# A linear-attention and MLP kernel: w spread by two TensorE row groups, unit 4 loaded ahead of w_out, score matmuls issued in pairs, and a new set of planner costs

## The chip, the cores and the metric

The kernel runs on one core of a Trainium2 chip. The core has five engines with their own instruction streams: TensorE (PE, with its weight loads shown as PEld), VectorE (DVE), ScalarE (ACT), GpSimd (POOL) and SyncE (SP), which here issues nearly all DMAs. They work on SBUF, on the PSUM banks that TensorE writes, and on device memory. The metric is the device time of one execution in microseconds (us), as a median of five runs.

## The reference

There are 4 x 8 heads with 768 time steps and a head dimension of 48. Per head a state is decayed by `w` and gains `k v` in each step; the output adds the current step with a weight `u`. The result goes through an MLP with the activation called smelu.

```python
for t in range(S):
    cur = einsum('bhd,bhe->bhde', u[None] * kt, vt)
    y[:, :, t] = einsum('bhd,bhde->bhe', rt, state + cur)
    state = w[None, :, :, None] * state + einsum('bhd,bhe->bhde', kt, vt)
x = y.transpose(0, 2, 1, 3).reshape(B * S, H * D)          # 3072 x 384
h = x @ w_in                                               # 384 -> 2048
g = where(h >= 1, h, where(h <= -1, 0, (h + 1) ** 2 / 4))
out = g @ w_out                                            # 2048 -> 384
```

## The kernel before, in words

**Units and blocks.** The time steps are cut in chunks of 128. A unit is one chunk of one batch entry, all 8 heads: 24 units, in the order of chunks. Two units make a block of 256 rows for the MLP: 12 blocks.

**Attention of a unit.** K and R (float32, 128 x 384) are scaled by powers of w, `Winv` and `Wpow`, into bf16 (`f_kw`, L447, and `f_rw`, L451). The scaled pair is transposed to `RK`: for the first 8 units by TensorE (L469) with a copy out of PSUM (`f_rk`), for the others by a transposing DMA on SP (L488). Scores are eight matmuls of 48 rows (`f_at`, L499), each in the lower or the upper half of the array's rows, into two PSUM buffers; DVE multiplies them with a triangular mask (`f_mask`, L505). The output y collects the carried state (L556, not for the first chunk) and scores times V (L559). The current step's weight comes from a product P and four small matmuls for the first 8 units (`f_p`, `f_dg`, L515 and L521) and from two products on POOL and a sum on DVE for the others (`f_ku`, `f_red`, L535 to L541). V times that weight (`f_vd`, L546) is added to y (`f_x`, L571). The result x is transposed into `xT`, by TensorE (L581) for 8 units and by DMA (L589) for the others. The state T gains four matmuls (`f_st`, L607), is decayed on POOL (L618) and cast to `Tbd`.

**MLP.** Layer 1 has eight groups per block, each six matmuls of 256 columns (`layer1`, L644) and one squaring activation on ACT (L656): the middle branch of smelu, for all elements. Layer 2 has four groups per unit, each four matmuls of 384 columns (`layer2`, L667); a copy out of PSUM and one output DMA follow (L690). Row norms of x and column norms of w_in (`f_sq` to `f_ws`, L707 to L724, and `f_b2` to `f_b4`) bound the largest |h|; if the bound is over the limit, a branch at the end does the MLP again in full (L759). It is not taken for these inputs.

**What sets the order.** All instructions are recorded as operations (`P.op`) with engines, planned durations, dependencies and a due time; `Plan.run` lists them greedily, and the program is issued in that order. The due times and their corrections (`CFG["due"]`, `CFG["bias"]`) are constants. MLP groups have a late due time, so they fill PE wherever attention has nothing to issue. Buffers come from pools (`slots`): for PSUM, four banks `a` for attention, two `h`, two `o`. The matmuls on `zero` (L357) are fillers at the start that compute nothing.

**Loads.** SP issues loads in the order of `CFG["order"]`: U is a unit's K, R and V, I a quarter of w_in, O a quarter of w_out (each weight quarter 768 KB in float32, cast to bf16 in three or four pieces at L284). Eight DMAs may be out at once.

**Preparing w.** `w_row` is loaded to one partition, ACT takes its logarithm there (L327), a matmul with ones spreads it over 128 partitions (`f_lwb`, L333), and two exponentials make Winv and Wpow (L359, L360).

Of the kernel before, what the change touches and what calls it, by code (L numbers as in the profile page):

```python
# [16 lines left out]
    "order": "U0 U1 U2 U3 I0 I1 I2 I3 O0 O1 O2 U4 O3 U5 U6 U7",  # L17
    "soft": 8,
    "sw": False,
    "due": [12.12, 22.15, 27.93, 36.84, 35.31],  # L20
    "step": 12.04,
    "warm": 24.0,
    "steady": 45.0,
    "slack": 0.19,
    "split": 2,
    "bias": {
        "at": 1.0, "bd": -4.91, "c_uw": 1.38, "dg": 0.1, "ku": -0.0, "kw": 1.96, "ldVf": 1.45, "red": -0.75,
        "rk": 0.3, "rkk": -6.72, "rkr": -0.29, "rw": 1.99, "st": 0.57, "t": -0.92, "trd": 0.24, "trk": -2.87,
        "trr": -3.35, "tw": -0.9, "v": -0.89, "x2": -1.05, "xt": 2.62, "y": -2.02,
    },  # L30
}


class Buf:
    def __init__(self, pool):
        self.pool, self.users, self.slot, self.t = pool, [], None, None


class Op:
    def __init__(self, name, engs, fn, deps, uses, allocs, due, dma, after, nb, late):  # L40
# [3 lines left out]
        self.eng = self.start = self.end = None  # L44
        for b in self.uses + self.allocs:
            b.users.append(self)


class Plan:
# [13 lines left out]
    def place(self, o):  # L63
        got, t = [], 0.0
        for b in o.allocs:
            best = None
            for i, cur in enumerate(self.slots[b.pool]):
                if any(g[0] == b.pool and g[1] == i for g in got):
                    continue
                if cur is None:  # L70
                    free = 0.0
                elif all(u.start is not None for u in cur.users):
                    free = max(u.end for u in cur.users) + SEM
                else:
                    continue
                if best is None or free < best[0]:
                    best = (free, i)
            if best is None:
                return None
            got.append((b.pool, best[1]))  # L80
# [3 lines left out]
    def run(self):  # L84
# [5 lines left out]
        while todo:  # L90
            cand, gone = [], []
            for o in todo:
                if any(d.start is None for d in o.deps) or any(a.start is None for a in o.after):
                    if o.late is not None and free["PE"] > o.late:
                        gone.append(o)
                    continue
# [15 lines left out]
            for o in gone:  # L112
                todo.remove(o)
                for b in o.uses:
                    b.users.remove(o)
            if not cand and gone:
                continue
# [70 lines left out]
def kernel(  # L188
# [163 lines left out]
    for i in range(160):  # L352
        def f_wm(e, i=i):
            if wmb.t is None:
                get(wmb, [128, 128], F32)
# [457 lines left out]
```

## Time and profile before

| what | value |
|---|---|
| median of five runs | 180.46 us (180.18 to 181.15) |
| profiled execution | 180.56 us |
| its span, first to last instruction | 178.6 us |
| PE, ACT, DVE, POOL busy | 168.8, 115.6, 112.0, 105.4 us |
| first layer-1 group | 18.56 us |
| end of the last matmul | 173.48 us |
| issue of the last output | 174.28 us |

Times in the timeline are us from the start of the span. A matmul's shown length includes its way through the array, so neighbours overlap; what a group costs PE is the distance from its start to the next start. An arrow in brackets names what ended the idle time before an instruction. Fillers count as busy.

### The profile page before, as it was taken

The numbers are of one execution on the slowest core, as the hardware profiler recorded it, in microseconds if no ns is written. First come the engines' busy times: TensorE is split into PE (matmuls) and PEld (weight loads), VectorE is DVE, ScalarE is ACT, GpSimd is POOL, SyncE is SP. The second block draws the span as 40 slices with busy tenths as digits, with TensorE's granted clock in tenths as the row PEclk, the third lists the DMA queues.
The fourth block names the chain that finished last, engine by engine and source line by source line (L and its number), as shares of the span: only waits on it lengthen the run. The fifth ranks groups of instructions, "written<-read, shape, count | busy, mean of one in ns | idle before, by whom it ended". The sixth has DMA issues, their size and how long they took to land.

```text
span 178.6 us, 4705 instructions
## 1 busy us (share of the span) xinstructions
PE 168.8 (94%) x1808; PEld 127.0 (71%) x1808; DVE 112.0 (63%) x221; ACT 115.6 (65%) x257; POOL 105.4 (59%) x142
## 2 busy tenths in 40 slices
PE   7899989999989999999999999989999999999980
PEld 7689967776767777777777767766767767777740
DVE  6699974598999795777758855746766634100000
ACT  4359987744476985884976766767685456645520
POOL 8659571387795999778599749579775510000000
PEclk9999999999999999999999999999999999999999
DMA  5999999997989959979899989889998782111111
GB/s 112 202 213 317 398 343 336 232 194 156 214 195 195 177 122 204 182 170 195 173 191 172 158 174 187 201 169 194 188 182 166 167 242 60 32 44 48 44 48 56
DMA packets 105920, 31.50 MB, mean 176 GB/s; under 512 B 98978, under 2 KB 104356, under 8 KB 105892
## 3 DMA queue, kind: packets, MB, share of 16 engines
q1 hardware_dynamic: 105744, 31.04, 78.4%
q8 instruction: 16, 0.26, 0.6%
q14 instruction: 12, 0.10, 0.2%
q10 hardware_dynamic: 148, 0.10, 0.2%
HBM read 20.65 MB, written 4.72 MB: 142 GB/s over the span
## 4 chain that ended last, share of the span: by engine, by line
PE 65%; DVE 12%; DMA 9%; ACT 4%; POOL 3%; issue 3%; SPq 1%; DVEq 0%; ACTq 0%; POOLq 0%
PE h L644 27%; PE o L667 27%; DMA RK<-KR 4%; PE a L499 3%; DMA R<-in_r_dram 3%; PE o L357 3%; DVE AT L505 3%; DMA out_dram<-os 3%; DVE VD L546 2%; DVE x L571 1%; PE a L559 1%; DVE KR L451 1%; PE a L556 1%; DVE w_in_sb L284 1%; DVE RK L284 1%
## 5 line engine op out<-in xcount | busy, mean ns | idle before, releaser
L644 PE MATMUL h<-xT,w_in_sb 128*128 128x256 bf16 x576 | 77.8, 273 | 1.0 <-DVE w_in_sb L284 0.4
L667 PE MATMUL o<-w_out_sb,g 128*128 128x384 bf16 x384 | 77.0, 326 | 0.0
L656 ACT ACTIVATE g<-h 128x512 bf16<-128x512 f32 x96 | 56.6, 595 | 27.9 <-PE h L644 26.6
L644 PEld LDWEIGHTS <-w_in_sb 128*128 128x128 bf16 x576 | 54.4, 98 | 15.0 <-issue 0.7
L667 PEld LDWEIGHTS <-g 128*128 128x128 bf16 x384 | 35.1, 98 | 15.5
L505 DVE TENSOR_TENSOR AT<-a,umask 128x512 bf16<-128x512 f32 x48 | 31.1, 683 | 8.6 <-PE a L499 8.4
L546 POOL TENSOR_TENSOR VD<-V,dg 128x384 f32<-128x384 bf16 x18 | 16.0, 892 | 11.9 <-DVE dg L541 8.3
L571 DVE TENSOR_TENSOR x<-a,VD 128x384 bf16<-128x384 f32 x24 | 13.3, 554 | 11.8 <-PE a L559 8.4
L536 POOL TENSOR_TENSOR KU<-KU,R 128x384 f32<-128x384 f32 x16 | 17.6, 1103 | 2.4 <-DMA R<-in_r_dram 1.3
L451 DVE TENSOR_TENSOR KR<-R,Wpow 128x384 bf16<-128x384 f32 x20 | 17.7, 887 | 2.1 <-DMA R<-in_r_dram 2.0
L535 POOL TENSOR_TENSOR KU<-K,u_bc 128x384 f32<-128x384 f32 x16 | 18.2, 1139 | 1.2 <-DMA K<-in_k_dram 1.1
L597 ACT ACTIVATE x<-x 128x384 bf16<-128x384 bf16 x24 | 12.5, 523 | 6.6 <-DVE x L571 6.2
L284 DVE COPY os<-o 128x384 f32<-128x384 f32 (+1 forms) x6 | 3.1, 521 | 19.9 <-ACT os L284 18.7
L618 POOL TENSOR_TENSOR T<-T,wc 128x192 f32<-128x192 f32 x20 | 12.0, 602 | 5.9 <-ACT T L284 4.0
L447 POOL TENSOR_TENSOR KR<-K,Winv 128x384 bf16<-128x384 f32 x11 | 11.0, 999 | 5.4 <-DMA K<-in_k_dram 4.6
L357 PE MATMUL o<-zero 128*128 128x128 bf16 x156 | 13.0, 236 | 1.0 <-DVE zero L321 1.0
L284 ACT COPY os<-o 128x384 f32<-128x384 f32 (+1 forms) x19 | 8.9, 470 | 6.7 <-PE o L667 3.6
L614 DVE TENSOR_TENSOR T<-T,a 48x192 f32<-48x192 f32 x32 | 11.2, 349 | 2.8 <-ACT g L656 1.1
L284 ACT CAST V<-Vf 128x384 bf16<-128x384 f32 x19 | 9.6, 507 | 4.6 <-DMA Vf<-in_v_dram 3.0
L447 DVE TENSOR_TENSOR KR<-K,Winv 128x384 bf16<-128x384 f32 x13 | 9.3, 713 | 4.2 <-DMA K<-in_k_dram 4.1
L284 ACT CAST Tbd<-T 48x192 bf16<-48x192 f32 x30 | 10.4, 347 | 2.0 <-PE a L556 1.2
L357 PEld LDWEIGHTS <-zero 128*128 128x128 bf16 x156 | 10.6, 107 | 1.2 <-DVE zero L321 1.0
(78 smaller groups left out, 174.0 us busy)
## 6 DMA issues: line engine op xcount, KB each, us to landing
K<-in_k_dram SPq DMA_DIRECT2D x24, 192.0 KB, 3.7
R<-in_r_dram SPq DMA_DIRECT2D x24, 192.0 KB, 4.1
Vf<-in_v_dram SPq DMA_DIRECT2D x24, 192.0 KB, 4.5
out_dram<-os SPq DMA_DIRECT2D x23, 192.0 KB, 2.3
wf<-in_moe_w_in_dram SPq DMA_DIRECT2D x4, 768.0 KB, 7.6
wf<-in_moe_w_out_dram SPq DMA_DIRECT2D x4, 768.0 KB, 8.9
RK<-KR SPq DMA_TRANSPOSE x16, 3.2
xT<-x SPq DMA_TRANSPOSE x16, 3.0
```

Of the source, the lines that this page charges most:

```text
L284: (nc.scalar.copy if eng == "ACT" else V_ENG[eng].tensor_copy)(o, i)
L357: mm(wmb.t, zero, zero, start=True, stop=True, skip_group_check=True)
L447: V_ENG[e].tensor_mul(krb.t[:, H:, 0:D], Kb.t, Winv)
L451: V_ENG[e].tensor_mul(krb.t[:, :H, 0:D], Rb.t, Wpow)
L505: nc.vector.tensor_mul(atb.t[s], at_p[s].t, umask4)
L535: nc.gpsimd.tensor_mul(kub.t, Kb.t, u3)
L536: nc.gpsimd.tensor_mul(kub.t, kub.t, Rb.t)
L546: V_ENG[e].tensor_mul(vdb.t, vb.t, dgb.t[:, :, None].to_broadcast([128, H, D]))
L571: nc.vector.tensor_add(xb.t, yb.t[:, 0:384].rearrange("p (h d) -> p h d", h=H), vdb.t)
L644: mm(hb.t[:, f, :], w_in_sb[:, kk, (2 * n + f) * 128 : (2 * n + f + 1) * 128], xT[m][:, kk, :], start=(kk == 0), stop=(kk == nKb - 1),)
L656: nc.scalar.activation(gb[m].t[:, 2 * n : 2 * n + 2, :], hb.t, AF.Square, bias=0.5, scale=0.5)
L667: mm(ob.t, gb[m].t[:, f, j * C : (j + 1) * C], w_out_sb[:, f, :], start=(f == 0), stop=(f == nN - 1))
```

## The change

The new version differs in these parts:

- **w.** Its two halves are loaded to partitions 0 and 64 (`w_sp`). Two matmuls, each in its own row group, spread w itself over 128 partitions; ACT takes the logarithm of the spread halves, then the two exponentials. The rows for the per-partition constants are made afterwards.
- **Load order.** Unit 4 comes ahead of the first quarter of w_out instead of ahead of the last: on SP, the issues after w_in's last quarter are K4, R4, O0, V4, O1, O2, O3, K5, R5; before they were O0, K4, O1, O2, R4, O3, V4, K5, R5.
- **Blocks whole** (`split` 0). In units 0 and 1 the transposes and copies of K and R are issued as one, no longer as two halves.
- **Transposes.** Units 8 and 9 also use TensorE for `RK` (`tpe` 10); the xT transposes and the P path stay with the first 8 units.
- **First unit in any bank.** Unit 0 may use PSUM banks of all three pools (`wide` 1); the planner picks the bank that is free first.
- **Masks.** One of the two masks of units 0 and 1 is taken from a bf16 copy that ACT makes out of PSUM.
- **Pairs.** From block 4 on, the score matmuls of a block's two units are issued as one operation of sixteen, which takes all four `a` banks.
- **Norms of w_in.** POOL adds the two halves of each squared pair into `mx`; eight small matmuls come in one place instead of sixteen in eight places, and start 30 us later.
- **Output.** The last unit's layer 2 is cut into columns 0 to 255 and 256 to 383, each with its own PSUM buffer, eviction and output on SP. Units 12 to 17 send their rows in two DMAs.
- **Fillers** have 256 columns instead of 128. **The fallback branch** is a loop over chunks.
- **Planner.** It has new durations (a slower DVE where POOL is busy, slower matmuls before 5.5 us), due times and corrections, so that the order of nearly all instructions changes a little.

```diff
-    "order": "U0 U1 U2 U3 I0 I1 I2 I3 O0 O1 O2 U4 O3 U5 U6 U7",
-    "soft": 8,
+    "order": "U0 U1 U2 U3 I0 I1 I2 I3 U4 O0 O1 O2 O3 U5 U6 U7",
+    "tpe": 10,
+    "dmm": 8,
+    "xpe": 8,
+    "pair": 4,
+    "cold": 5.5,
+    "am0": 0,
+    "am1": 2,
+    "norm": 100.0,
+    "wide": 1,
-    "due": [12.12, 22.15, 27.93, 36.84, 35.31],
-    "step": 12.04,
+    "due": [6.87, 37.3, -17.41, 33.54, 38.54],
+    "step": 11.06,
-    "slack": 0.19,
-    "split": 2,
+    "slack": 0.05,
+    "split": 0,
...
-    zero = const.tile([128, 128], BF16, name="zero")
-    w_row = const.tile([1, H * D], F32, name="w_row")
+    zero = const.tile([128, 256], BF16, name="zero")
+    w_sp = const.tile([128, H * D // 2], F32, name="w_sp")
...
+    def f_wb(e):
+        for s in range(2):
+            get(wbb[s], [128, H // 2, D], F32)
+            mm(wbb[s].t, onesf[s * DP : s * DP + 1, :], w_sp[s * DP : s * DP + 1, :], start=True, stop=True)
+    c_wb = P.op("c_wb", {"PE": (0.45, 0.55)}, f_wb, deps=[c_wr, c_z], allocs=wbb, due=-98)
+    lws = [slice(s * H // 2, (s + 1) * H // 2) for s in range(2)]
+
+    def f_lw(e):
+        for s in range(2):
+            nc.scalar.activation(lw[:, lws[s]], wbb[s].t, AF.Ln)
...
-            for _ in range(2):
-                mm(wmb.t, zero, zero, start=True, stop=True, skip_group_check=True)
+            mm(wmb.t, zero[:, 0:128], zero, start=True, stop=True, skip_group_check=True)
...
+        A = "a h o" if i < CFG["wide"] else "a"
+        by_pe, by_mm, x_pe = i < CFG["tpe"], i < CFG["dmm"], i < CFG["xpe"]
...
+            if i < CFG["am%d" % s]:
+                amb = Buf("am")
+
+                def f_am(e, s=s, amb=amb):
+                    get(amb, [128, NP, 128], BF16)
+                    nc.scalar.copy(amb.t, at_p[s].t)
+                o_am = P.op(f"am{s}_{i}", act(512), f_am, deps=[o_at], uses=[at_p[s]], allocs=[amb], due=D0 - 3)
+
+                def f_mask(e, s=s, amb=amb):
+                    nc.vector.tensor_mul(atb.t[s], amb.t, umaskb4)
...
+        if m >= CFG["pair"]:
+            def f_at2(e, got=got):
+                for x in got:
+                    x[0](e)
+            o = P.op(f"at_{m}", pe(0.63), f_at2, deps=got[0][1] + got[1][1], uses=[x[2] for x in got], allocs=got[0][3] + got[1][3], due=got[0][4])
+            ats = [o, o]
...
+        cuts = [(0, d_out)] if i < NU - 1 else [(0, 256), (256, d_out)]
+        rows_ = [(0, C)] if i not in TWICE else [(0, C // 2), (C // 2, C)]
...
+            for k, (r0, r1) in enumerate(rows_):
+                def fo(e, lo=lo, hi=hi, r0=r0, r1=r1):
+                    nc.sync.dma_start(out=out[t0 + r0 : t0 + r1, lo:hi], in_=osb.t[r0:r1, lo:hi])
...
+            nc.gpsimd.tensor_add(mx[n // 2], ssb.t[:, 0:128], ssb.t[:, 128:256])
...
+    def f_np(e):
+        get(npb, [128, nP], F32)
+        for g in range(nP):
+            mm(npb.t[:, g : g + 1], mx[g], ones, start=True, stop=True)
...
+        with tc.For_i(0, NCH, 1) as ci:
```

## The prediction

> **What bounds the kernel now.** I read the page's busy line first, then its slices, then the chain of waits, and last TensorE's timeline.
>
> ```profile
> span 178.6 us, 4705 instructions
> PE 168.8 (94%) x1808; PEld 127.0 (71%) x1808; DVE 112.0 (63%) x221; ACT 115.6 (65%) x257; POOL 105.4 (59%) x142
> ...
> PE   7899989999989999999999999989999999999980
> ...
> DMA  5999999997989959979899989889998782111111
> ```
>
> PE is the busy engine, and the DMA engines are full for the first quarter. But a busy PE early on is partly filler: the matmuls on `zero` (L357) compute nothing. So I went through PE's timeline:
>
> ```profile
> 0.99 3.17 PE L357 MATMUL o<-zero 128*128 128x128 bf16 x28 [0.99 <-DVE zero L321]
> 4.09 1.18 PE L333 MATMUL a<-rows,onesf 1*128 1x384 f32 x2
> ...
> 18.56 0.82 PE L644 MATMUL h<-xT,w_in_sb 128*128 128x256 bf16 x6
> ...
> 25.81 2.33 PE L644 MATMUL h<-xT,w_in_sb 128*128 128x256 bf16 x18 [0.37 <-ACT w_in_sb L284]
> ...
> 35.77 0.82 PE L667 MATMUL o<-w_out_sb,g 128*128 128x384 bf16 x4
> ```
>
> The first layer-1 group starts at 18.56, the groups then wait for the casts of w_in (25.81), and the group at 35.77 is the first that uses the last quarter of w_out. The transfers set these, as the casts that waited for them show:
>
> ```profile
> 26.06 0.70 POOL L284 CAST w_out_sb<-wf 128x384 bf16<-128x384 f32 x1 [1.07 <-DMA wf<-in_moe_w_out_dram]
> 28.95 0.70 POOL L284 CAST w_out_sb<-wf 128x384 bf16<-128x384 f32 x1 [2.19 <-DMA wf<-in_moe_w_out_dram]
> 31.55 0.70 POOL L284 CAST w_out_sb<-wf 128x384 bf16<-128x384 f32 x1 [1.90 <-DMA wf<-in_moe_w_out_dram]
> 34.66 0.51 POOL L284 CAST w_out_sb<-wf 128x384 bf16<-128x384 f32 x1 [2.41 <-DMA wf<-in_moe_w_out_dram]
> ```
>
> So w_out's quarters land at 26.0, 28.9, 31.5 and 34.6. After 35.77 PE is the bound, and only less work or fewer waits on it help. The steps are read from start to next start:
>
> ```profile
> 146.84 0.81 PE L644 MATMUL h<-xT,w_in_sb 128*128 128x256 bf16 x6
> 147.59 0.40 PE L499 MATMUL a<-RK 48*128 48x128 bf16 x8
> 147.92 0.82 PE L667 MATMUL o<-w_out_sb,g 128*128 128x384 bf16 x4
> 148.58 0.60 PE L644 MATMUL h<-xT,w_in_sb 128*128 128x256 bf16 x4
> ```
>
> An MLP group steps 0.65 us (147.92 to 148.58). The group ahead of the 48-row score matmuls (L499) steps 0.75, so going into them costs 0.10, and the eight step 0.33: 0.43 for a unit. The same reading gives 0.44 for a unit's eight transposes, 0.11 for dg, 0.17 each for st, xp and the carried state in y, 0.20 for y's own eight. Last, the tail:
>
> ```profile
> 173.54 0.32 ACT L284 COPY os<-o 128x192 f32<-128x192 f32 x1 [2.12 <-PE o L667]
> 173.89 0.38 ACTq L690 DMA_DIRECT2D out_dram<-os  x1
> 173.89 0.36 DVE L284 COPY os<-o 128x192 f32<-128x192 f32 x1 [18.66 <-ACT os L284]
> ```
>
> PE ends at 173.48; the two half evictions run one after the other, and the last output is issued at 174.28. The execution took 180.56 (1.96 outside its span), 0.10 above the median 180.46; my sum starts from 180.56.
>
> **The change, part by part.**
>
> *Start.* Before, w lands at 2.19, its logarithm ends at 2.71, but the broadcast matmuls stand behind 28 fillers until 4.09, and Winv ends at 5.89. After, five fillers of 256 columns come first, then two row groups spread w itself (L333 took 1.03 for twice the columns: 0.5 side by side, which I take, 1.0 one after the other), then two half logarithms on ACT (about 0.34 each, from 0.52 for 384 columns) and the exponentials (0.58): Winv at about 4.5, 1.4 earlier. Then I followed the new order by DVE, which has kw and rw of units 0 and 1 (0.55 each where POOL is idle, 1.27 where it is not), RK1 0.69, masks 0.68 or 0.42 from a bf16 copy, P 0.42, x 0.55: x of unit 0 ends at 13.9 (before 13.99), unit 1 at 16.35 (17.17), its transposed copy, behind a mask and a w_in cast, at 17.85. First layer-1 group at 18.0, not 18.56: R1 lands at 6.5 and the w_in casts end at 17.8, so most of the 1.4 is lost to loads. Larger fillers cost nothing: they stand where PE waits anyway.
>
> A row bears on the early matmuls: the 28 fillers step 0.113 us, those after 5 us 0.056, while the page's granted clock shows full speed throughout. The Trainium skill (TensorE: Matmul & The Clock Gate, Part 1: The HAM clock gate) says that an array just woken runs at half clock for about 3.4 us; the fillers' steps agree, and it speaks against moving the broadcast from 4.09 to 2.2; by it the two would take 1.03 and not 0.5, and Winv would end at 5.0. The sum would not move by either, since R1 and w_in come later still.
>
> *Four units, then w_in, then unit 4, then w_out.* The first sixteen loads keep their order, so w_in's last quarter still lands at about 23.8 and the seventh layer-1 group can start at 24.6 (before 25.81). Unit 4's three loads now stand ahead of w_out's last three quarters, where two stood before. Single loads follow each other by 0.7 to 1.0 us, so the last quarter lands at about 35.4 instead of 34.6, its casts take 1.0 as before, and the group of 35.77 starts at 36.4. From 24.6 PE has ten layer-1 groups, three layer-2 groups (8.45) and unit 4 (1.69): done by 35.3, with 0.5 for the wait on R. About 1.1 us of waiting is thus new. In return dg, st, the carried state, y and xp of unit 4 (0.82) lie behind. Net gain at this point 0.82 - 0.63 = 0.2.
>
> *PE work from there on.* Both have 173 MLP groups left: 112.45. Before: transposes of three units 1.32, scores 19 x 0.43 = 8.17, dg 0.44, st 2.72, carried state 3.40, y 4.00, xp 0.68, norms and b3 0.67. Sum 133.85, against 137.71 measured: 3.9 us of waits. After: units 8 and 9 also go through PE, so transposes are 5 x 0.44 = 2.20. Scores of blocks 4 to 11 are issued in pairs: eight matmuls in two row groups side by side need 4 x 0.055 (a transpose's step) = 0.22, so 0.11 of the 0.33 and the 0.10 before it are the cost of going in and out; a pair pays it once: 0.21 + 2 x 0.22 = 0.65 instead of 0.86. Scores: 3 x 0.43 + 8 x 0.65 = 6.5. dg 0.33, st 2.55, carried 3.23, y 3.80, xp 0.51, norms in one place and b3 0.42. Sum 132.0. No row shows a pair; between no saving (0.86) and 0.65 I take 0.65, since each of 14 score groups in steady state shows the 0.10. So before, 35.77 + 133.85 + 3.9 = 173.5; after, if the waits stay 3.9, 36.4 + 132.0 + 3.9 = 172.3: 1.2 earlier (1.85 less work, of which 0.8 had been done before 36.4, and 0.6 lost at the start).
>
> *Waits.* The longest of the old ones are for transposing DMAs (0.4 to 0.5), an output buffer at 115 and the row norms at 132.8. Two transposing DMAs fewer and one place of norms speak for less; four PSUM buffers taken at once by a pair, and six outputs split in two (six more issues of 0.4 to 0.6 on SP, with the loads queued behind) for more. Bounds -2 to +4; I take 0. The masks through ACT (units 0 and 1), P, and the norms on POOL run on engines that idle there; if that cover fails, the masks cost ACT 0.6 each. First units in any bank cannot cost once layer 1 starts; before, it only removes waits.
>
> *Tail.* One eviction of 128 columns (about 0.27, from 0.32 for 192) stands between the last matmul and the last issue, in place of 0.80: -0.4. The split layer 2 is 16 x 0.108 + 16 x 0.055 = 2.61 against 2.60. The fallback branch becomes a loop and doesn't run: 0, within 0.5 both ways.
>
> Sum: 180.56 - 1.2 - 0.4 = 178.96; less the 0.10 by which that execution lies above the median, 178.9. That is my prediction.
>
> **The rivals.**
> 1. Slower: a pair needs all four `a` buffers. PE runs in order, so it stands until every mask, copy and x of earlier units has freed them, with MLP groups queued behind. For it: masks are 0.68 each and DVE is 63% busy. Against: about 2 us of MLP groups lie around each pair. Eight waits of one mask, 5.4 us, give 184.3; from 0.21 us a pair the gain is gone, from 0.27 it is slower.
> 2. No change: w_out comes later by all three of unit 4's loads, 2.4 us instead of 0.8. For it: the DMA engines are full there; against: two of the three were ahead of the last quarter before. 178.9 + 1.6 = 180.5.
> 3. Larger gain: the waits halve (3.9 to 2.0) because two transposing DMAs leave the full stretch: 177.0. Against: DVE is at 9.2 of 10 us from 50 to 60.
> 4. Row groups don't run side by side: Winv 0.5 later, hidden by loads, so still 178.9.
>
> **How the numbers follow.** My forecast with rival 4 has 0.50 (its own range 177.9 to 179.9), rival 1 0.20, rival 2 0.15, rival 3 0.15. A measurement of this kernel tells about 0.3% from no change: under 179.92 or over 181.0. Faster: 0.50 + 0.15 + a little of rival 2 = 0.66; same 0.14; slower 0.20. The range takes rival 3 to its middle and rival 1 up to 0.38 us a pair: 176.9 to 181.9.
>
> **What would show it.** First layer-1 group at about 18.0; the fourth layer-2 group, after a wait for w_out's cast, at 36 to 37; pairs stepping 0.55 with 0.75 for the group ahead; PE's end near 172.3; 0.4 from there to the last issue. I am wrong if groups ahead of pairs step far over 0.75 (rival 1), if w_out's last cast ends past 37.5 (rival 2), or if PE waits elsewhere from 36 to 60, where DVE is nearly full.

## The result: no faster, and the profile after

| | kernel before | changed kernel |
|---|---|---|
| median of all executions, us | 181.15 (79) | 182.23 (42) |
| lowest to highest, us | 179.18 to 184.05 | 178.98 to 184.41 |
| ratio, 95% interval | | 1.0013 (0.9988 to 1.0037) |
| profiled execution, us | 180.56 | 182.91 |
| its span, us | 178.6 | 181.0 |

The forecast was 178.9, 0.85% faster. The measurement shows no gain, and by the medians of all executions the changed kernel is 0.6% slower. Single executions of either kernel scatter by some 1.5% and fall into a faster and a slower state: the ratio compares the faster ones alone (median 181.05 for the changed kernel), and of its two profiled executions the one here, 182.91, is of the slower ones, the second, 182.67 (h3_after, in the last group of runs), of the faster. The second profile has its marks within 0.2 us of the first. The two profiled executions in the table lie 2.35 us apart, the medians 1.1.

The first lines of the page of the changed kernel, and its chain of work that ended last:

```profile
PE 170.1 (94%) x1762; PEld 128.9 (71%) x1762; DVE 111.7 (62%) x218; ACT 118.4 (65%) x261; POOL 105.7 (58%) x147
...
PE h L717 32%; PE o L751 31%; PE o L406 5%; PE a L537 3%; PE a L611 2%; DVE AT L555 2%; DVE P L567 2%; PE a L507 2%; DMA RK<-KR 2%; DVE VD L598 2%; PE a L608 2%; DMA w_sp<-in_w_dram 1%; PE a L659 1%; DVE x L623 1%; DVE KR L489 1%
```

PE is as busy as before. New is the third entry of the chain: 5% of it, some 8 us, are fillers (L406), which compute nothing; 7.2 of these lie in the first 24 us. TensorE's timeline (start, us, engine, line, operation, what it waited for) shows where they stand:

```profile
3.48 1.01 PE L369 MATMUL a<-w_sp,onesf 1*128 1x192 f32 x4 [1.16 <-DMA w_sp<-in_w_dram]
4.42 2.74 PE L406 MATMUL o<-zero 128*128 128x256 bf16 x12
7.08 1.01 PE L391 MATMUL a<-onesf,rows 1*128 1x1 f32 x8
8.03 1.03 PE L507 MATMUL a<-ident,KR 128*128 128x128 bf16 x8
8.85 1.70 PE L406 MATMUL o<-zero 128*128 128x256 bf16 x7
...
11.55 0.47 PE L537 MATMUL h<-RK 48*128 48x128 bf16 x8
...
12.88 2.14 PE L406 MATMUL o<-zero 128*128 128x256 bf16 x18
16.28 0.25 PE L573 MATMUL a<-uw,P 128*128 128x2 bf16 x4 [1.25 <-DVE P L567]
...
23.12 0.81 PE L717 MATMUL h<-xTa,w_in_sb 128*128 128x256 bf16 x6
```

The twelve fillers step 0.21 us from start to start, the eighteen later ones 0.11: up to about 11.7 us the array works at half rate. In the kernel before, its one-column matmuls step 0.06 from 5.1 on, here 0.11: there full rate had come by then. The first scores (L537) start at 11.55, the first layer-1 group at 23.1 instead of 18.56. The kernel before had its first scores at 10.10:

```profile
10.10 0.40 PE L499 MATMUL a<-RK 48*128 48x128 bf16 x8
```

Which of these rows follow on one another is told by the chain of waits of the first 24 us (start, us, what):

```profile
0.79 2.55 DMA w_sp<-in_w_dram
...
4.48 2.67 PE o L406 x12
...
9.06 1.49 PE o L406 x7
...
13.85 1.24 DVE AT L552
15.09 2.14 DVE P L567 x2
...
20.12 1.20 PE o L406 x11
```

Fillers are links of this chain, then a mask (1.24 us for a 0.43 us operation) and two products P (2.14 us for 0.84). Fillers are links again from 18.9 to 23.0, 2.8 us of them, now at full rate. These stand mostly where TensorE would wait: the last input of the first layer-1 group, unit 1's transposed x, is copied by 22.5 (0.35 us from 22.16 on VectorE), so that the fillers and scores behind that copy can have held the group back by at most 0.6. ScalarE's queue shows why w is late: issuing the two-partition load took 1.11 us (first line, changed kernel), against 0.53 for the one-partition load (second line, kernel before).

```profile
0.79 1.11 ACTq L329 DMA_DIRECT2D w_sp<-in_w_dram  x1
0.77 0.53 ACTq L294 DMA_DIRECT2D w_row<-in_w_dram  x1
```

Late in the kernel the pairs step as forecast, 0.55, and the group ahead of each steps 0.75. Two of the eight pairs have a wait inside (0.74 and 1.00). One of the other six:

```profile
61.76 0.82 PE L717 MATMUL h<-xTa,w_in_sb 128*128 128x256 bf16 x6
62.51 0.62 PE L537 MATMUL a<-RK 48*128 48x128 bf16 x16
63.06 0.82 PE L751 MATMUL o<-w_out_sb,g 128*128 128x384 bf16 x4
```

### The profile page after: what moved, and what is told of

Same layout as the page of the kernel before. It is cut to its first block, busy times and chain, and to the rows that moved or that the text cites. A ratio compares the mean times of both kernels' runs of the same rounds, so it can differ in the third digit from the quotient of the medians.

```text
span 181.0 us, 4588 instructions
## 1 busy us (share of the span) xinstructions
PE 170.1 (94%) x1762; PEld 128.9 (71%) x1762; DVE 111.7 (62%) x218; ACT 118.4 (65%) x261; POOL 105.7 (58%) x147
## 4 chain that ended last, share of the span: by engine, by line
PE 79%; DVE 12%; DMA 3%; ACT 1%; issue 1%; POOL 0%
PE h L717 32%; PE o L751 31%; PE o L406 5%; PE a L537 3%; PE a L611 2%; DVE AT L555 2%; DVE P L567 2%; PE a L507 2%; DMA RK<-KR 2%; DVE VD L598 2%; PE a L608 2%; DMA w_sp<-in_w_dram 1%; PE a L659 1%; DVE x L623 1%; DVE KR L489 1%
## 5 line engine op out<-in xcount | busy, mean ns | idle before, releaser
L717 PE MATMUL h<-xTa,w_in_sb 128*128 128x256 bf16 x576 | 76.8, 272 | 1.3 <-DMA xTa<-x 1.0
L751 PE MATMUL o<-w_out_sb,g 128*128 128x384 bf16 (+2 forms) x400 | 75.7, 320 | 0.0
L751 PEld LDWEIGHTS <-g 128*128 128x128 bf16 x400 | 36.6, 98 | 15.7
L555 DVE TENSOR_TENSOR AT<-a,umask 128x512 bf16<-128x512 f32 x45 | 28.3, 683 | 14.2 <-PE a L537 14.0
L598 POOL TENSOR_TENSOR VD<-V,dg 128x384 f32<-128x384 bf16 x19 | 15.9, 838 | 18.0 <-DVE dg L593 8.0
L489 DVE TENSOR_TENSOR KR<-R,Wpow 128x384 bf16<-128x384 f32 x22 | 16.7, 758 | 1.0 <-DMA R<-in_r_dram 0.8
L623 DVE TENSOR_TENSOR x<-a,VD 128x384 bf16<-128x384 f32 x24 | 13.3, 554 | 4.2 <-PE a L611 3.8
L406 PE MATMUL o<-zero 128*128 128x256 bf16 x84 | 14.5, 316 | 1.1 <-DVE zero L358 1.1
L319 ACT COPY os<-o 128x384 f32<-128x384 f32 (+2 forms) x21 | 9.7, 463 | 7.5 <-PE o L751 6.9
L319 ACT CAST Tbd<-T 48x192 bf16<-48x192 f32 x36 | 12.5, 346 | 2.2 <-POOL T L670 1.9
L593 DVE TENSOR_REDUCE dg<-KU 128x8 f32<-128x384 f32 x16 | 8.7, 546 | 7.1 <-POOL KU L588 7.0
L802 POOL TENSOR_TENSOR ss<-sq 128x256 bf16<-128x256 bf16 x8 | 5.7, 708 | 10.6 <-ACT sq L793 10.6
L406 PEld LDWEIGHTS <-zero 128*128 128x128 bf16 x84 | 8.5, 111 | 3.4 <-DVE zero L358 1.1
```

Source lines behind the costliest of these rows:

```text
L319: (nc.scalar.copy if eng == "ACT" else V_ENG[eng].tensor_copy)(o, i)
L406: mm(wmb.t, zero[:, 0:128], zero, start=True, stop=True, skip_group_check=True)
L489: V_ENG[e].tensor_mul(krb.t[:, :H, 0:D], Rb.t, Wpow)
L555: nc.vector.tensor_mul(atb.t[s], at_p[s].t, umask4)
L598: V_ENG[e].tensor_mul(vdb.t, vb.t, dgb.t[:, :, None].to_broadcast([128, H, D]))
L623: nc.vector.tensor_add(xb.t, yb.t[:, 0:384].rearrange("p (h d) -> p h d", h=H), vdb.t)
```

## The experiments

For every run I read four marks in TensorE's timeline: the first scores, the first layer-1 group, the fourth layer-2 group (the first that needs the last quarter of w_out), and PE's end (the end of its last matmul). "Rest" is from the fourth layer-2 group to PE's end. Times are medians of all executions of that batch, with the kernel before beside it; the ratio is against the kernel before.

| run | first scores | first L1 | fourth L2 | PE's end | rest | median (n) | before (n) | ratio, 95% |
|---|---|---|---|---|---|---|---|---|
| before | 10.10 | 18.56 | 35.77 | 173.48 | 137.7 | | | |
| h4_before | 9.97 | 18.4 | 36.0 | 172.1 | 136.1 | 179.90 (1) | 180.77 (11) | |
| after | 11.55 | 23.12 | 40.34 | 176.56 | 136.2 | 182.23 (42) | 181.15 (79) | 1.0013 (0.9988 to 1.0037) |
| h3_after | 11.54 | 23.25 | 40.44 | 176.39 | 136.0 | 183.31 (4) | 180.77 (11) | 1.018 (1.011 to 1.025) |
| e1_drop20 | 9.75 | 22.14 | 39.25 | 174.98 | 135.7 | 181.08 (10) | 181.64 (25) | 1.0014 (0.9967 to 1.0061) |
| e2_ahead5 | 11.26 | 22.98 | 40.33 | 177.02 | 136.7 | 182.00 (10) | 181.64 | 1.008 (1.002 to 1.014) |
| e3_onerow | 9.16 | 20.90 | 38.02 | 175.86 | 137.8 | 181.77 (10) | 181.64 | 1.007 (1.001 to 1.013) |
| e4_apart | 11.69 | 23.40 | 40.75 | 178.49 | 137.7 | 183.75 (4) | 181.64 | 1.017 (1.006 to 1.027) |
| f1_order | 11.55 | 21.94 | 39.06 | 174.32 | 135.3 | 182.42 (4) | 181.02 (25) | 1.012 (1.003 to 1.022) |
| f2_ahead14 | 11.38 | 22.90 | 40.02 | 175.84 | 135.8 | 181.65 (10) | 181.02 | 1.005 (1.000 to 1.011) |
| f3_order14 | 9.70 | 22.39 | 39.75 | 175.99 | 136.2 | 181.04 (10) | 181.02 | 1.005 (1.000 to 1.011) |
| f4_orderrow | 8.96 | 20.91 | 39.76 | 176.49 | 136.7 | 181.26 (10) | 181.02 | 1.0012 (0.9963 to 1.0061) |
| g1_late | 11.02 | 22.76 | 39.96 | 174.23 | 134.3 | 180.90 (4) | 180.60 (13) | 1.012 (1.001 to 1.023) |
| g2_new | 9.49 | 21.72 | 38.87 | 174.46 | 135.6 | 179.84 (10) | 180.60 | 1.0002 (0.9946 to 1.0059) |
| g2_again | 9.48 | 21.56 | 38.71 | 174.96 | 136.3 | 180.78 (12) | 180.42 (17) | 1.005 (1.001 to 1.010) |
| g3_newsp | 10.04 | 22.15 | 39.30 | 176.88 | 137.6 | 181.43 (4) | 180.60 | 1.011 (0.998 to 1.025) |
| h2_skip | 11.58 | 21.22 | 38.34 | 175.24 | 136.9 | 180.15 (1) | 180.77 | |
| h1_new2 | 9.48 | 18.30 | 42.56 | 178.26 | 135.7 | 184.11 (6) | 180.77 | 1.020 (1.014 to 1.026) |
| i1_new3 | 9.49 | 18.21 | 41.30 | 177.25 | 135.9 | 183.60 (12) | 181.57 (17) | 1.009 (1.005 to 1.013) |
| i2_new4 | 9.48 | 18.14 | 41.99 | 177.12 | 135.1 | 183.91 (6) | 180.42 | 1.024 (1.019 to 1.030) |

The rest lies between 134.3 and 137.8 whatever was edited at the start, and for the unedited kernels too (137.7 and 136.1 in two profiles of the one before). The same changed kernel gave 1.0013 in one batch and 1.018 in a batch of four. So a time of few executions can't tell effects under 1 us, and the verdicts below go by the marks. Each mark is of one execution: the two profiles of the changed kernel agree within 0.2, but where the moment of full rate differs the start moves by up to 1.9 (g1_late below). All edits keep the planner's list and change it, or a body, only when it is written out.

**Theory and rivals.** A: the fillers hold up the work behind them in TensorE's queue, at half rate above all. B: they only fill waits, and VectorE and GpSimd set the start. C: without them the array stays slow.

**e1_drop20: the fillers ahead of the first scores away.**

```diff
-    for o in P.run():
+    seq = P.run()
+    seq = [o for o in seq if o.name not in [f"wm{i}" for i in range(5, 25)]]
+    for o in seq:
```

> The changed kernel, its order kept, without the 20 fillers (256 columns each) that stand in TensorE's queue between the spread of w and the first scores (12 + 7 + 1, in its profile at 4.42 to 7.08, 8.85 to 10.35 and 11.20 to 11.55 us). Theory A, the fillers hold up the work behind them: the transposes of the u columns start when their rows are there (6.6, not 7.08), the second unit's transposes at about 8.9 (not 10.35), the first scores at about 9.7 (not 11.55), and with VectorE 1.8 us earlier from there the first layer-1 group comes at about 21.3 (not 23.1) and the time falls by 1 to 1.8 us. Theory B, they only fill waits and VectorE's and GpSimd's shared work sets the start: first layer-1 group within 0.4 of 23.1, the time the same. Theory C, they keep the array's clock up: without them the transposes and scores stay at half rate longer and the first layer-1 group comes later.

```profile
6.67 1.01 PE L391 MATMUL a<-onesf,rows 1*128 1x1 f32 x8 [2.16 <-ACT rows L379]
...
9.75 0.61 PE L537 MATMUL h<-RK 48*128 48x128 bf16 x8 [0.24 <-ACT RK L319]
...
11.90 4.02 PE L406 MATMUL o<-zero 128*128 128x256 bf16 x18
```

A holds for the first scores, 1.8 us earlier to within 0.1. The eighteen fillers that remain step 0.21, at half rate up to 15.9, and now stand ahead of a product that is ready. So the first layer-1 group gains 1.0, PE's end 1.6; the time does not differ from the kernel before. Whether the array stayed slow for so long because fillers were missing (C) is not shown by one execution: the moment of full rate moves without an edit too (g1_late below).

**e2_ahead5 and f2_ahead14: fillers moved ahead of the spread of w.**

```diff
+    for i in range(5, 10):
+        move(f"wm{i}", "c_wb")
```

```diff
+    for i in range(5, 14):
+        move(f"wm{i}", "c_wb")
+    k = seq.index(at["wm16"])
+    seq[k:k] = [at["wm15"]] * 13
```

> The changed kernel with five of the twelve fillers that follow the spread of w moved ahead of it, so that TensorE does not stand still from 2.3 to 3.5 us; as many fillers as before. If the pause is what keeps the array at half rate until about 11 us: full rate from about 4.1 us (as the unbroken fillers of the kernel before show), the spread 0.5 us, the later fillers 0.11 each, first scores at about 9 (not 11.55), first layer-1 group at about 20.6, time 1.5 to 2.5 us less. If the rate does not depend on the pause: only the five moved fillers (5 x 0.22 = 1.1 us) leave the queue ahead of the u columns, which then wait for their rows (6.6), and the gain is 0.5 us at most.

> The changed kernel with nine of the twelve fillers moved ahead of the spread of w, so that 14 fillers run unbroken from 1.07 to about 4.2 us, and 13 more fillers behind it to keep TensorE busy up to the u columns. If the array reaches full rate after about 3.1 us of matmuls over all its rows, as the 28 fillers of the kernel before do (0.99 to 4.09), and the one-row matmuls of the spread had broken that off: spread at 4.2 and 0.5 long, fillers 0.11 each behind it, transposes 0.45, first scores at about 9 (not 11.55), first layer-1 group at about 21.0 (not 23.1). If full rate comes at a fixed time from the start, or after the first transposes whatever came before: no change of the first scores beyond 0.5.

f2_ahead14 also puts thirteen more fillers behind the spread. The pause of TensorE at 2.3 us is not what keeps the rate down: with all but 0.45 us of it filled, fillers still step 0.21 to beyond 13 us, and the first three marks stay within 0.3. Nor do fourteen unbroken fillers ensure full rate: f2_ahead14 has no pause of TensorE from 1.07 to beyond 9 us, and half rate lasted to 9.4. The next two fences are f2_ahead14 and f3_order14 (below), whose instructions are the same up to the transposes:

```profile
1.07 3.17 PE L406 MATMUL o<-zero 128*128 128x256 bf16 x14 [1.07 <-DVE zero L358]
4.17 1.01 PE L369 MATMUL a<-w_sp,onesf 1*128 1x192 f32 x4
5.11 3.59 PE L406 MATMUL o<-zero 128*128 128x256 bf16 x16
```

```profile
4.17 0.88 PE L369 MATMUL a<-w_sp,onesf 1*128 1x192 f32 x4
4.98 1.92 PE L406 MATMUL o<-zero 128*128 128x256 bf16 x16
```

The sixteen fillers behind the spread step 0.21 in one execution and 0.11 in the other.

**e3_onerow: w in one partition, no row groups.**

```diff
-    c_wr = ... nc.scalar.dma_start(out=w_sp[0:128:64, :], in_=w.rearrange("(s h) d -> s (h d)", s=2)) ...
+    c_wr = ... nc.scalar.dma_start(out=w_row, in_=row(w)) ...
...
-            mm(wbb[s].t, onesf[s * DP : s * DP + 1, :], w_sp[s * DP : s * DP + 1, :], start=True, stop=True)
+            mm(wbb[s].t, onesf[0:1, :], w_row[:, s * (H * D // 2) : (s + 1) * (H * D // 2)], start=True, stop=True)
```

> The changed kernel with w loaded into one partition as in the kernel before and spread by two matmuls from that one row, one after the other; all else in its order. This undoes the row groups alone. If w's late landing and the pause of TensorE that it makes cost the start: w at 2.0 (not 3.3), the spread from about 2.3 without a pause before it, Winv at about 4.0 (not 5.07), full rate from about 4.1, first layer-1 group 2 to 3 us earlier and the time 1 to 2.5 us less. If two matmuls side by side were worth it: Winv no earlier than 5.0 and the time the same or up to 0.5 more.

```profile
2.25 1.64 PE L369 MATMUL a<-w_row,onesf 1*128 1x192 f32 x4
3.82 2.74 PE L406 MATMUL o<-zero 128*128 128x256 bf16 x12
...
9.16 0.40 PE L537 MATMUL h<-RK 48*128 48x128 bf16 x8
```

The load was issued in 0.51 us and the spread began 1.23 earlier. From one row it took 1.57 (2.25 to 3.82), from two row groups 0.94: these do run side by side, but the late landing costs more than they save, and Winv starts at 4.29 instead of 5.07. Full rate came at 7.0, the first layer-1 group 2.2 earlier, the fourth layer-2 group 2.3, PE's end only 0.7, since this execution has a rest of 137.8.

**g1_late: the one-row kernel without the late fillers.**

```diff
+    seq = [o for o in seq if not (o.name.startswith("wm") and o.start > 18.0)]
```

> w in one partition as in the one-row run, and besides without the fillers that stand behind the first layer-1 group's place and just ahead of it (from 18 us of the written order on: 8 + 2 stand between the first layer-1 groups at 22.6 and 25.1 of that run's profile, 1.1 us). If they hold up layer-1 groups that are ready: from the first layer-1 group (20.9) to the fourth layer-2 group 16.1 us instead of 17.1, which then comes at about 37, and the time falls by about 1 us against the one-row run. If the loads and casts of w_in and w_out set that stretch: fourth layer-2 group at 38 as before, no gain.

From the first layer-1 to the fourth layer-2 group it takes 17.2 us, as with the fillers: these do fill waits, for casts and evacuations. But this run tells more. Its first 17 us are written as in e3_onerow, and yet:

```profile
3.88 2.74 PE L406 MATMUL o<-zero 128*128 128x256 bf16 x12
...
8.32 1.70 PE L406 MATMUL o<-zero 128*128 128x256 bf16 x7
...
13.18 2.17 PE L406 MATMUL o<-zero 128*128 128x256 bf16 x18
```

Full rate came at 13.3, not 7.0, and the first layer-1 group at 22.76, not 20.90. So 1.9 us of the start are the moment of full rate, which is not the program's. Most of e3_onerow's gain is therefore that moment. Against the changed kernel, whose two profiles had full rate at 11.7 and 12.6, g1_late's first layer-1 group is only 0.4 to 0.5 earlier; that is what w's earlier landing is worth, as far as one execution shows it.

**h2_skip: VectorE without GpSimd beside it.** GpSimd's rw2, kw3 and rw3 are left out, so units 2 and 3 lack these values.

```diff
+    at["rw2"].fn = at["rw3"].fn = lambda e: None
+    at["kw3"].fn = lambda e: setattr(at["kw3"].allocs[0], "t", KR[at["kw3"].allocs[0].slot])
```

> The changed kernel without GpSimd's three products of units 2 and 3 that stand beside VectorE's masks and products of units 0 and 1 (rw2, kw3 and rw3, at 13.8 to 17.1 us in the profile after); the output lacks these units' keys and receptances. If the shared work slows VectorE: the second bf16 mask 0.43 (not 1.24) and the two products P 0.42 each (not 1.17), so that from the first scores to the first layer-1 group it takes 9.3 us instead of 11.6. If VectorE's order alone makes that stretch long: 11 or more.

VectorE's timeline of the changed kernel, then of this run:

```profile
13.85 1.24 DVE L552 TENSOR_TENSOR AT<-am,umaskb 128x512 bf16<-128x512 bf16 x1
15.01 2.35 DVE L567 TENSOR_TENSOR P<-RK 128x512 bf16<-128x512 bf16 x2
```

```profile
13.84 0.42 DVE L552 TENSOR_TENSOR AT<-am,umaskb 128x512 bf16<-128x512 bf16 x1
14.18 0.75 DVE L567 TENSOR_TENSOR P<-RK 128x512 bf16<-128x512 bf16 x2
```

The first scores are at 11.58 as before, the first layer-1 group at 21.22: 9.6 us between them instead of 11.6. It is the cleanest result of the study: 1.9 us of the start are GpSimd's work beside VectorE's. That units 2 and 3 need not wait for their own values here is no rival: in the changed kernel none of TensorE's waits before 23 us is for GpSimd. The Trainium skill (GPSIMD Engine Reference, 1. Specifications) says that the two engines' SBUF interface is shared and contends with VectorE instructions that have two SBUF inputs; the rows agree, since P and the mask from the bf16 copy take 2.5 to 3 times as long and the mask from PSUM (0.68 beside GpSimd) does not. GpSimd's timeline of the changed kernel shows how:

```profile
13.81 1.00 POOL L489 TENSOR_TENSOR KR<-R,Wpow 128x384 bf16<-128x384 f32 x1
14.76 1.17 POOL L485 TENSOR_TENSOR KR<-K,Winv 128x384 bf16<-128x384 f32 x1
15.90 1.17 POOL L489 TENSOR_TENSOR KR<-R,Wpow 128x384 bf16<-128x384 f32 x1
```

Each of the three VectorE operations starts just after one of these has started, and ends 0.28 us after that one's end (15.09, 16.22 and 17.36 after 14.81, 15.94 and 17.08). So it is not slower throughout, it is held until GpSimd's operation is done. In f1_order a P that starts 0.29 ahead of a GpSimd product takes its 0.42.

**f1_order, f3_order14 and f4_orderrow: products ahead of masks.**

```diff
+    behind("v0", "P0")
+    behind("at0", "dg0")
+    behind("am1_0", "dc0")
+    behind("kw2", "rw2")
+    behind("mask1_0", "P1", "vd0")
+    behind("wm33", "y0", "x0")
+    behind("wm39", "tr2", "xp0")
```

A name is an operation and its unit: `P0` is the product P of unit 0, `at0` its scores. f3_order14 adds the edit of f2_ahead14, f4_orderrow that of e3_onerow.

> The changed kernel with the first two units' work in another order and nothing else: the products P of units 0 and 1 stand ahead of the masks on VectorE (behind v0, and behind the first unit's masks), dg0, its copy, vd0, y0 and x0 follow at once, and GpSimd does rw2 ahead of tw0. Theory D, the order on VectorE costs the start (P at 15.0 to 17.4 us in the profile after, 1.17 us each beside GpSimd's kw and rw, 0.42 each in the kernel before): P0 at about 10.4, x0 at about 14.6 (not 18.5), first layer-1 group at about 20.7 (not 23.1). Theory A alone (TensorE's cold queue sets all of it): first layer-1 group within 0.6 of 23.1. For the time, 1 to 2 us less under D, none under A.

> Both edits, the order of the first two units and the 14 fillers ahead of the spread. If the start was lost by these two and the gain behind it is real, first layer-1 group at about 18.5, fourth layer-2 group at 36.5 to 37.5 (the last quarter of w_out lands at 36.05 in the profile after), PE's end at about 172.5 to 173.5 and the time 178 to 179.5: about the forecast. If the loads give the block-0 time back: fourth layer-2 group at 38 or later, time within 1 us of the changed kernel.

> The new order of the first two units together with w in one partition (no row groups), fillers as in the changed kernel. The one-row start alone had the first layer-1 group at 20.90. If the two causes add: about 18.5, fourth layer-2 group 36.5 to 37.5, time 178 to 179.5. If VectorE is what both wait for, so that they overlap: 20 to 20.5, time about 180.

The order alone gains half of what was expected (21.94, not 20.7). VectorE's sum for x of unit 0 starts 3.6 earlier (14.91, not 18.50), that for unit 1, which the group needs too, only 1.2 (19.58, not 20.76): GpSimd still holds up one P and one mask (1.02 and 1.11), and I had put unit 0's transposes ahead of unit 1's work, where they wait for x. In f3_order14, with full rate at 4.8 and the first scores at 9.70, that wait is longest:

```profile
15.96 0.34 PE L633 MATMUL h<-ident,x 128*128 128x128 bf16 x3 [1.45 <-DVE x L623]
```

Its first layer-1 group came at 22.39, not 18.5 as expected, and later than in f1_order. With w in one partition the order gains nothing more either: 20.91 against the 20.90 of e3_onerow. The causes do not add. In f4_orderrow w_out's last quarter landed at 38.74, and the fourth layer-2 group waited for its cast:

```profile
39.76 2.11 PE L751 MATMUL o<-w_out_sb,g 128*128 128x384 bf16 x12 [1.49 <-DVE w_out_sb L319]
```

In the other runs it landed between 35.5 and 37.8 and this wait is absent. So the loads are next in line: an earlier start helps only down to about the landing plus 1 us (39.76 after 38.74 in this one execution).

**e4_apart: the pairs taken apart.**

```diff
+            if m >= CFG["pair"] and j == 1:
+                mm(at_p[0].t[:, 0, 0:32], zero[:, 0:128], zero[:, 0:32], start=True, stop=True)
             for p in range(NP):
```

> The changed kernel with a matmul over all 128 rows (32 columns) put between the two units of each of the eight pairs of scores, so that the array leaves the half-row mode and enters it again once more a pair. If the pairs' saving is on the path that sets the end: 8 x (0.21 + about 0.05) = 2.1 us more. If waits had hidden it: under 0.5 us more.

```profile
62.91 0.40 PE L539 MATMUL a<-RK 48*128 48x128 bf16 x8
63.24 0.19 PE L536 MATMUL a<-zero 128*128 128x32 bf16 x1
63.37 0.40 PE L539 MATMUL a<-RK 48*128 48x128 bf16 x8
63.70 0.82 PE L753 MATMUL o<-w_out_sb,g 128*128 128x384 bf16 x4
```

Two units now take 0.79 instead of 0.55: 0.24 a pair, 1.9 in all. The rest, 137.7, does not decide, since e3_onerow has 137.8 without this edit; nor does the time (1.017, against 1.0013 and 1.018 of the unedited kernel). PE's busy time within the rest does: 135.9 us, against 134.0 and 133.9 in the two profiles of the changed kernel and 133.4 to 135.0 in all its other variants. The 1.8 to 2.0 more agree with the step, and PE stands still for only 1.9 of the 137.7: the pairs' saving is real and on the path.

**g2_new, g3_newsp and g2_again: a new order of the first four units.** The list is sorted anew with 29 operations given other places (products ahead of masks, v0 and vd0 to GpSimd, two copies to ScalarE), and most fillers are left out; g3_newsp has w over two partitions.

```diff
+    when = {
+        "P0": 8.17, "dg0": 8.3, "dc0": 8.85, "rw2": 9.05, "vd0": 9.06, "mask0_1": 9.6, "P1": 9.62, "y0": 9.63,
...
+    for n, e in (("v0", "POOL"), ("vd0", "POOL"), ("dc1", "ACT"), ("xt1", "ACT")):
+        at[n].eng = e
...
+    seq.sort(key=lambda o: o.start)
```

> w in one partition, and the first four units' work written in a new order: products ahead of masks, v0 and vd0 to GpSimd, two small copies to ScalarE, x1 and its transposes ahead of units 2 and 3, and two fillers of three left out from 10 us on, all from 18. This asks whether the first layer-1 group can stand at the 18.0 of the forecast, and what the whole kernel then takes. If the start is all that failed in the forecast: first layer-1 group at 17.5 to 18.5, fourth layer-2 group at the last landing of w_out (36 to 37.5) plus about 1, PE's end 172 to 173.5, time 178 to 179.5. If the start is worth little because w_out's landing and the casts on VectorE come next: fourth layer-2 group at 38 or later, time 180 to 181.

> The same new order with the two row groups of the changed kernel (w over two partitions). Against the run with w in one partition it shows what the row groups cost in an order that is not held up elsewhere: if w's later landing (3.3, not 2.0) and the half rate that it brings pass through, the first scores are 2 us later and the first layer-1 group 1 to 2 us later; the time follows by as much only if the fourth layer-2 group does too, and by nothing where w_out's landing sets it.

> The kernel of g2_new once more, for its time beside the kernel before on another chip: 0.3 to 0.6 us under the kernel before by the medians if that run's difference was real, none if it was chance. Its profile should show the fourth layer-2 group at 38 to 39 again, with the moment of full rate between 6 and 13.5 us.

The first layer-1 group came at 21.6 to 21.7, since scores that waited for a copy stood ahead of it. g2_new was 0.8 us under the kernel before by the medians, its repetition 0.4 over: no gain is shown. In both profiles the array fell back to half rate for 3.4 us (from 16.7 and 16.5 on). The row groups cost 0.5 at the first scores and 0.4 at the first layer-1 group (one execution each), less than expected.

**h1_new2, i1_new3 and i2_new4: the first layer-1 group where the forecast had it.** Each takes the last obstacle of the run before it away: L1_0_0, the first layer-1 group, ahead of unit 3's scores (first two lines below); fillers kept (next two); the second and third groups ahead too (last three).

```diff
+        "P2": 11.05, "xp1": 10.98, "xt1": 11.02, "at2": 11.15, "cI02": 12.2, "cI00": 12.25,
+        "tr3": 11.3, "cI01": 12.35, "rk3": 12.4, "L1_0_0": 12.5, "g0_0": 12.6,
...
+    for i in range(36, 48):
+        at[f"wm{i}"].start = 10.97 if i < 40 else 12.45
...
+        "g0_0": 12.6, "L1_0_1": 12.61, "g0_1": 12.62, "st2": 12.63, "dg2": 12.64, "dc2": 12.65, "t2": 12.66, "vd2": 12.7,
+        "y2": 12.75, "at3": 13.58, "x2": 13.36, "cI12": 13.38, "cI10": 13.39, "cI11": 13.4,
+        "L1_0_2": 13.6, "g0_2": 13.65,
```

> w in one partition and the new order of the first four units once more, with the second unit's transposes ahead of the third unit's scores, the casts of w_in's first quarter ahead of units 2 and 3 on VectorE and GpSimd, and the first layer-1 group ahead of the scores of unit 3. In the run before it, the first layer-1 group (21.72) had its columns ready at 18.5 and stood behind scores that waited for a copy. If the start is all that failed in the forecast: first layer-1 group at 18.5 to 19.5, fourth layer-2 group at 37 to 38 (w_out's last quarter lands at 36 to 37), PE's end at 173 to 174, median 179 to 179.5. If units 2 and 3 give it back: fourth layer-2 group at 39 again and the median at 179.8 as in that run.

> w in one partition and the order of h1_new2, with the fillers kept up to the first layer-1 group and behind it (placed ahead of what waits: the second unit's products and transposes, and the first layer-1 group). If too few fillers were what made that run slow: layer-1 groups of 0.65 us from the first one on, first layer-1 group at 18.3 to 19, fourth layer-2 group at 37 to 38.5, PE's end at 173 to 174.5 and the median at 179 to 180. If the order of units 2 and 3 is what made it slow: groups of 0.65, but the fourth layer-2 group at 39 or later and the median above 180.5.

> As i1_new3, with the second and third layer-1 groups, their evacuations, unit 2's outputs and the casts of w_in's second quarter ahead of the scores of unit 3, and that unit's state copied earlier. If the fourth layer-2 group follows the start once nothing waits: first groups at 18.3, 19 and about 21.5 (w_in's second quarter lands at 20), the seventh at 25 to 26, the fourth layer-2 group at 37 to 38.5, PE's end at 173 to 174.5 and the median at 179 to 180. If the work that is moved back (units 3 to 5) takes it again: fourth layer-2 group at 39 or later, median above 180.5.

In h1_new2 the group stands at 18.30, but the array has fallen back to half rate, from 18.3 to 21.7 and from 25.1 to 32.0:

```profile
18.30 1.46 PE L717 MATMUL h<-xTa,w_in_sb 128*128 128x256 bf16 x6 [0.62 <-POOL w_in_sb L319]
...
29.47 2.68 PE L717 MATMUL h<-xTa,w_in_sb 128*128 128x256 bf16 x12
```

With the fillers kept, i1_new3 still fell back, from 24.4 to 27.8. i2_new4, with the next groups moved too, did not, but there other links are missing. Its timeline of TensorE:

```profile
22.91 0.83 PE L717 MATMUL h<-xTa,w_in_sb 128*128 128x256 bf16 x6 [1.63 <-DVE w_in_sb L319]
...
26.68 0.33 PE L659 MATMUL a<-V,KR 128*128 128x96 bf16 x4 [1.63 <-ACT V L319]
```

The casts and copies that I had moved back for the first group are now late for the third. From the first layer-1 to the fourth layer-2 group it takes 23 to 24 us instead of 17.2, and these runs are 0.9 to 2.4% slower than the kernel before. So the first group's time is a mark, not a cause; pulled forward alone, it gave nothing in any of the three.

**h3_after and h4_before: both kernels once more.**

> The changed kernel itself once more, for a second profile and for times beside the others on the same chip. If the moment of full rate is set by the program: fillers at 0.22 us until 11 us again and the first layer-1 group at 23.1. If it is free against the program: another moment, between 5 and 13.5 us, and the first layer-1 group earlier or later by about as much as the first scores.

> The kernel before itself once more, for a second profile. Its 28 fillers stand unbroken ahead of its first matmul on w, which came at 4.09 with the array at full rate. If the moment of full rate is free against the program: fillers behind it at 0.11 us instead of 0.066 and full rate up to 3.4 us later, and the first layer-1 group later than 18.56. If unbroken fillers fix it: full rate at 4.1 again.

The changed kernel reached full rate at 12.6 (11.7 in its first profile), the kernel before at 4.4 (4.7 in its first profile), within its two one-row matmuls:

```profile
4.09 1.05 PE L333 MATMUL a<-rows,onesf 1*128 1x384 f32 x2
4.98 0.60 PE L341 MATMUL a<-onesf,rows 1*128 1x1 f32 x8
```

No version is shown to be faster than the kernel before.

## Why the prediction was wrong, step by step

The sum failed at one term, the start: *"First layer-1 group at 18.0, not 18.56"*. Against the profiled execution (182.91, forecast 178.96): first layer-1 group at 23.1 instead of 18.0, +5.1; from there to the fourth layer-2 group 17.2 instead of 18.4, -1.2; the rest 136.2 instead of 135.9, +0.3; from PE's end to the end of the execution 6.3 instead of 6.7, -0.3. That is +3.9, all from the start. Two smaller parts are not the kernel's: this execution lies 0.7 over the median of all, and the sum set out from a median of five (180.46), where that of 79 executions is 181.15. Three steps of the reckoning made the start wrong.

*"Larger fillers cost nothing: they stand where PE waits anyway."* I took each filler at 0.11 us and looked at where PE waited in the kernel before. At half rate twelve take 2.7 and seven 1.5, and the chain of waits runs through them. e1_drop20 shows 1.8 us at the first scores and 1.0 at the first layer-1 group.

*"The sum would not move by either"* (half rate or not). I weighed half rate for the two spread matmuls alone, 0.5 us. It lasted until 11.7 and 12.6 in the two profiles, and slowed fillers, transposes and scores. The same head with full rate 6 us earlier had its first layer-1 group 1.9 earlier (e3_onerow against g1_late).

*"masks 0.68 or 0.42 from a bf16 copy, P 0.42"*. P's 0.42 came from a row of the kernel before at which GpSimd was idle (it had nothing from 8.2 to 10.8); that kernel has no mask from a copy, and I gave it P's time.

```profile
10.10 0.42 DVE L515 TENSOR_TENSOR P<-RK 128x512 bf16<-128x512 bf16 x1
```

I had read kw and rw both with and without GpSimd (0.55 and 1.27) and did not do the same for masks and P: 1.24 and about 1.1 each, 1.9 us by h2_skip. *"The masks ..., P, and the norms on POOL run on engines that idle there"* named the cover and missed that it wasn't there.

Besides, I kept w's landing (2.2); over two partitions it was 3.3, and Winv ended at 5.68 instead of 4.5. By g1_late against the changed kernel and g3_newsp against g2_new this is worth 0.4 to 0.5 at the first layer-1 group. Rival 4 is settled: the groups do run side by side (0.94 against 1.57 at half rate).

The three causes overlap; their sizes, measured apart and in one or two executions each, are 1.0 to 1.8, 1.9 and 1.9 us, and no run has all removed with the rest in order. So that the start failed is shown, how the 5.1 divide among them is not. Whether the changed kernel with a mended start reaches 178.9 stays open; what is shown is that without GpSimd's part alone PE ends 1.3 earlier and one execution took 180.15.

*Loads* held: w_in's last quarter landed at 24.1 (forecast 23.8), w_out's at 36.05 (35.4). The layer-2 group did not wait for it because PE was already later; had the start held, it would have by the forecast's own reckoning. *PE work* held, with six of eight pairs at 0.55 and the groups ahead at 0.75, as did *Tail*: 0.3 us from PE's end to the last issue, 0.4 forecast. *Waits* of 3.9 (4.2 by the same subtraction from the rest) can't be judged from one profile, since the rest varies by 3.5 us between profiles; the second profile of the kernel before has 2.2.

Rival 1 (PE stands before each pair) fell: the groups ahead of pairs step 0.75. Rival 2 named w_out for a result near no change; the result came, by the start. No rival gave a price to a later start: rival 4, the one about it, called the delay hidden by loads.

## What to carry to other kernels

Read the durations of a new order from rows with the same neighbours: the same clock state, and the same engine at work beside it. An instruction that only fills time must be priced at the slowest rate that it can meet and at the place where it stands in an in-order queue; look in the chain of waits after the change for work that computes nothing. An operation that another engine holds up is priced by when that engine's operation ends, not by a factor. Where a kernel's first stage feeds a long one, forecast the start by its last link, not by the first: in h1_new2 to i2_new4 each link that was pulled forward left the next one where it was, or later.

## What the runs showed of the hardware

- The moment at which TensorE reaches full rate moves between executions of the same instructions: 7.0 and 13.3 us (e3_onerow, g1_late), 4.8 and 9.4 (f3_order14, f2_ahead14), 11.7 and 12.6 (the changed kernel). The steps of equal matmuls show it (0.21 and 0.11 for a filler); the profile's granted clock reads full speed there too, because its record begins at this moment. The Trainium skill (TensorE: Matmul & The Clock Gate, Part 1: The HAM clock gate) says that the window that decides is free-running, so that the same kernel has different numbers of slow matmuls; the runs agree. It also gives about 3.4 us of sustained work to full rate; here half rate lasted to 11 to 13 us in the changed kernel, though TensorE had been at work since 1.07 with pauses of about 1 us, on fillers, one-row matmuls and transposes, and to 9.4 in f2_ahead14 without a pause. What of these doesn't count as work was not tried; the kernel before, with 28 unbroken fillers ahead of its one-row matmuls, had full rate at 4.7 and 4.4 in its two profiles, f2_ahead14, with 14 of twice the width, did not.
- It falls back within the kernel: with two of three fillers left out, layer-1 groups ran at half rate from 18.3 to 21.7 and from 25.1 to 32.0 us (h1_new2), and here the granted clock shows it (0.50). No single pause ahead of the falls in h1_new2, i1_new3, g2_new and g2_again was over 1.6 us; in the 3.4 us ahead of each, TensorE had been busy for 1.4 to 1.9.
- A load of 2 x 192 values to two partitions took 1.11 us to issue, the same 384 values to one partition 0.51 to 0.53.
- Two-input bf16 operations of VectorE beside GpSimd: 1.24 instead of 0.42 (mask), 1.1 instead of 0.4 (P). Where GpSimd's operation had started first, VectorE's ended 0.28 us after it. A cast of V from float32, with one input, was held up too (1.15 instead of 0.35, at 9.18 in the changed kernel).
- Taking a pair of half-row matmul groups apart with a full-row matmul cost 0.24 us.
